# An attention and MLP kernel: other slots for the tile preparation, q turns ahead of their copies, and a last tile in three pieces

## The chip, the cores and the metric

The kernel runs on one core of a Trainium2 chip. The metric is the device time in microseconds (us), the median of several executions. All times below are in us unless marked ns.

## What is computed

Eight batches of attention without a softmax, each of 576 rows and 8 heads of 64, are normalised and go through a two-layer perceptron with a residual:

```python
kv = np.einsum('bhsd,bhse->bhde', k, v)
out = np.einsum('bhsd,bhde->bhse', q, kv)
rms = np.sqrt(np.mean(out * out, axis=-1, keepdims=True) + 1e-06)
x = (out / rms * g_norm)              # then heads side by side: (8, 576, 512)
xn = (x - mu) / np.sqrt(var + 1e-06) * g_ln
return x + np.maximum(xn @ w_ch1, 0.0) @ w_ch2     # 512 -> 2048 -> 512
```

The kernel computes in bf16 with f32 sums, and applies the 1/sqrt(var) of the second norm only at the end (`rstd`, in the output step), since it commutes with the relu.

## The kernel before, in words

**Work and tiles.** A batch has 576 rows: four row tiles of 128 (`main_tile`) and a remainder of 64. The remainders of two batches make one tile (`rem_tile`, made with the odd batch), and the four remainder tiles make a ninth block, "rem", computed last. A block of four tiles (512 rows) goes through the first product `mm1` (L391: 64 matmuls of 128x128 weights against 512 columns, with the relu on ScalarE, L404) and the second product `mm2` (L438, 16 matmuls for each of four row tiles, then `finish`, L420: the output step `o_sb` on VectorE, then two output DMAs on SP).

**Preparation of a tile** (class `Tile`, `plan_tile` L359). It comes in four parts, each put into a slot: first (`o`: four matmuls of q with kv, L259; `sq`: squares on ScalarE, L265; `red`: sum over the head on VectorE, L286), second two slots later (`root` on ScalarE L296, `inv`, `y`, `x`, `xc` on VectorE, L303, L291, L310, L320), third six slots after the first (`var`: the squares of the deviations on ScalarE, L328), and fourth the turn of xc into xT, the operand of `mm1` (L331): on TensorE with a copy on ScalarE for the early batches, by a transposing DMA on SP (L340) for batches 3 to 7.

**Slots and the order of work.** All engines run what they are given in the order of the program (`manual_schedule`, L62). `tick` (L460) counts slots: one slot is four matmuls of 512 columns, or as many of fewer columns as make the same work. Each `tick` first runs what `at` has put into its slot, in the order of the slot number and, where that is equal, in the order in which it was put there; then come the slot's own matmuls and their relu. Each block takes 16 slots of `mm1` and 16 of `mm2`, so batch b starts in slot s = 32 b. The preparation of batch b runs in the slots of batch b-1: `mm1` of b-1 is s-32 to s-17, `mm2` of b-1 is s-16 to s-1. The output step of the first of the four row tiles of `mm2` is emitted just ahead of slot s-12, the second ahead of s-8, the third ahead of s-4. The second product's sums `p2` have two PSUM buffers (`ps2`), the relu's inputs `p1` have three (`ps1`), the attention outputs two (`ps_out`, tag "ops").

For batches 3 to 7, `kv_of` of batch b is in slot s-39, and `turn_q_dma` in slot s-38: a copy of q on VectorE (L201) and one transposing DMA on SP (L203). Loads of later batches stand on GpSimd's queue.

**The start.** Batch 0 is special. Its kv comes from `kv_first`; its first two tiles are computed ahead of slot 0 in two halves of the heads (`half_o` L485, `half_sq`, `half_red`), with q turned on TensorE (`turn_groups`, L177) and copied out by ScalarE in the first half and by VectorE in the second; `fill` (L193) are matmuls on zeros. w1 and w2 arrive in four quarters each (`load_w1`, `load_w2`, GpSimd's queue). The first slots' products use the first two quarters of w1 (`mm1(0, ts, 1, 0, 8)` for tiles 0 and 1), slots 4 and 5 the third, 6 and 7 the fourth.

**The end.** The last row tile of the "rem" block is computed in two column halves (`split_last`), so that the output step and the output DMAs of the first half run beside the matmuls of the second; the two DMAs of each go out on SP and on ScalarE's queue.

Of the kernel before, what the change touches and what calls it, by code (L numbers as in the profile page):

```python
# [14 lines left out]
def kernel(  # L15
# [11 lines left out]
    nc = tc.nc  # L27
    f32 = mybir.dt.float32
    bf16 = mybir.dt.bfloat16
    AF = mybir.ActivationFunctionType  # L30
    ALU = mybir.AluOpType
    AX = mybir.AxisListType

    B, H, S, D = q.shape
    Dm = H * D
# [3 lines left out]
    nDe = Dh // 128  # L39
    HP = H // 2  # L40
# [11 lines left out]
    work = ctx.enter_context(tc.tile_pool(name="work", bufs=3))  # L52
# [4 lines left out]
    ps_out = ctx.enter_context(tc.psum_pool(name="ps_out", bufs=2))  # L57
    ps1 = ctx.enter_context(tc.psum_pool(name="ps1", bufs=3))
    ps2 = ctx.enter_context(tc.psum_pool(name="ps2", bufs=2))
# [7 lines left out]
    g_ln_sb = consts.tile([128, Dm], f32)  # L67
    gn_row = consts.tile([128, D], f32)
    identity = consts.tile([128, 128], bf16)
# [6 lines left out]
    kv_pack = [consts.tile([128, HP, 128], bf16, name=f"kv_pack{i}") for i in range(4)]  # L76
# [87 lines left out]
    qts, held, blks, rstds, m1s, q_ps = {}, {}, {}, {}, {}, {}  # L164
# [12 lines left out]
    def turn_groups(tp, i, h0, h1):  # L177
        groups = ((0, 2 * i), (0, 2 * i + 1)) if i < 2 else ((64, 2 * i - 4), (64, 2 * i - 3))
        if i == J:
            groups = ((0, J),)  # L180
        for h in range(h0, h1):
            for half, (p0, j) in enumerate(groups):
                nc.tensor.transpose(
                    tp[h % 2 * D:h % 2 * D + D, (h - h0) // 2, half * 64:half * 64 + 64],
                    q_in[0][p0:p0 + 64, h, j, :], identity[p0:p0 + 64, p0:p0 + 64])
        return 64 * len(groups)
# [162 lines left out]
    def rem_tile(b):  # L349
        mms = []  # L350
        for half, bb in enumerate((b - 1, b)):
            qt, kp = qts.pop(bb), held.pop(bb)
            mms.append((slice(half * 64, (half + 1) * 64),
                        lambda hp, qt=qt: qt[:, J, hp, :64], kp))
        if "rem" not in blks:
            blks["rem"] = new_block("rem", 1)
        return Tile(mms, blks["rem"], b // 2)

    def plan_tile(s, make, turn_at, on_pe):  # L359
        box = []  # L360

        def first():
            t = make()
            box.append(t)
            t.o()
            t.sq()
            t.red()

        def second():
            t = box[0]  # L370
            t.y()
            t.x()
            t.xc()

        def third():
            box[0].var()

        def fourth():
            box[0].turn(on_pe)

        at(s, first)
        at(s + 2, second)
        at(s + 6, third)
        at(turn_at, fourth)
# [28 lines left out]
    def mm2_part(b, ts, p2, de0, de1, c0=0, c1=Dm):  # L413
        for de in range(de0, de1):
            if de % 4 == 0:
                tick()
            nc.tensor.matmul(p2[:, c0:c1], lhsT=m1s[b][:, de, ts * 128:(ts + 1) * 128],  # L417
                             rhs=w2_sb[:, de, c0:c1], start=(de == 0), stop=(de == nDe - 1))

    def finish(b, ts, p2, c0=0, c1=Dm, both=False):  # L420
        o_sb = outp.tile([128, Dm], f32, tag="osb", name="o_sb")
        nc.vector.scalar_tensor_tensor(o_sb[:, c0:c1], in0=p2[:, c0:c1],  # L422
                                       scalar=rstds[b][:, ts:ts + 1],
                                       in1=blks[b][0][:, ts, c0:c1], op0=ALU.mult, op1=ALU.add)
        if b == "rem":
            dsts = [out[2 * ts + hf, :S_LO, :].rearrange("(p j) e -> j p e", j=JJ)[J]
                    for hf in range(2)]
        elif b == 0:
            dsts = [(out[b, :S_LO, :].rearrange("(p j) e -> j p e", j=JJ)[j] if ts < 2 else
                     out[b, S_LO:, :].rearrange("(p j) e -> j p e", j=J)[j - J])  # L430
                    for j in (2 * ts, 2 * ts + 1)]
        else:
            dsts = [out[b, :S_LO, :].rearrange("(p j) e -> j p e", j=JJ)[ts],
                    out[b, S_LO:, :].rearrange("(p j) e -> j p e", j=J)[ts]]
        nc.sync.dma_start(dsts[0][:, c0:c1], o_sb[:64, c0:c1])
        (nc.scalar if both else nc.sync).dma_start(dsts[1][:, c0:c1], o_sb[64:, c0:c1])

    def mm2(b, split_last=False):  # L438
        for ts in range(4):
            if split_last and ts == 3:  # L440
                for c0 in (0, Dm // 2):
                    p2 = ps2.tile([128, Dm], f32, tag="p2", name="p2")
                    mm2_part(b, ts, p2, 0, nDe, c0, c0 + Dm // 2)
                    finish(b, ts, p2, c0, c0 + Dm // 2, both=True)
                    del p2
            else:
                p2 = ps2.tile([128, Dm], f32, tag="p2", name="p2")
                mm2_part(b, ts, p2, 0, nDe)
                finish(b, ts, p2)
                del p2  # L450
        del blks[b], m1s[b]
# [5 lines left out]
    def at(slot, fn):  # L457
        agenda.setdefault(int(slot), []).append((slot, fn))
# [19 lines left out]
    t = [main_tile(0, i) for i in range(4)]  # L478
    for i in range(2):
        t[i].ss = work.tile([128, H, 1], f32, tag="ss", bufs=4, name="ss")  # L480
    sqs = [work.tile([128, H, D], f32, tag="sq", name="sq") for _ in range(2)]
    banks = (((ps_out, "ops"), (ps_m, "misc")), ((ps_out, "ops"), (ps1, "p1")))
    copies = ((nc.scalar.copy, nc.scalar.copy), (nc.vector.tensor_copy, nc.vector.tensor_copy))

    def half_o(half):  # L485
        hp0 = half * HP // 2
        tp = ps2.tile([128, 2, HP // 2, 128], bf16, tag="p2", name="tp")
        for i in range(2):
            turn_groups(tp[:, i], i, 2 * hp0, 2 * hp0 + H // 2)
            copies[half][i](qts[0][:, i, hp0:hp0 + HP // 2], tp[:, i])  # L490
        res = []
        for i in range(2):
            pool, tag = banks[half][i]
            o = pool.tile([128, H // 2, D], f32, tag=tag, name="o_half")
            flat = o.rearrange("p h e -> p (h e)")
            for k2 in range(HP // 2):
                nc.tensor.matmul(flat[:, k2 * 128:(k2 + 1) * 128], lhsT=qts[0][:, i, hp0 + k2, :],
                                 rhs=kv_pack[0][:, hp0 + k2, :], start=True, stop=True)
            res.append(o)
        return res  # L500

    def half_sq(i, half, o):
        nc.scalar.activation(sqs[i][:, half * H // 2:(half + 1) * H // 2], o, func=AF.Square)

    def half_red(i, half):
        hs = slice(half * H // 2, (half + 1) * H // 2)
        nc.vector.tensor_reduce(t[i].ss[:, hs], sqs[i][:, hs], axis=AX.X, op=ALU.add)

    oa = half_o(0)
    half_sq(0, 0, oa[0])  # L510
    half_sq(1, 0, oa[1])
    ob = half_o(1)
    half_sq(0, 1, ob[0])
    half_sq(1, 1, ob[1])
    for half in range(2):
        half_red(0, half)
    half_red(1, 0)
    half_red(1, 1)
    del oa, ob, sqs
    t[0].o_g(ps1, "p1")  # L520
    t[1].o_g(ps1, "p1")
    fill(5)
    t[0].x_g()
    t[1].root()
    x_blk, st, xT = t[0].blk
    for i in range(2):
        cs = slice(i * Dm // 2, (i + 1) * Dm // 2)
        xc = work.tile([128, Dm // 2], bf16, tag="xch", bufs=2, name="xc")
        nc.vector.scalar_tensor_tensor(xc, in0=x_blk[:, 0, cs], scalar=st[:, 1, 0:1],
                                       in1=g_ln_sb[:, cs], op0=ALU.add, op1=ALU.mult)  # L530
        tp = ps_out.tile([128, 2, 128], bf16, tag="ops", name="tp")
        for kk in range(2):
            nc.tensor.transpose(tp[:, kk, :], xc[:, kk * 128:(kk + 1) * 128], identity)
        nc.scalar.copy(xT[:, 2 * i:2 * i + 2, :128], tp)
        del xc, tp
    t[1].x_g()
    t[1].xc()


    def x2():  # L540
# [19 lines left out]
        load_batch(2)  # L560

    at(0, lambda: turn_first(2, ps_m, "misc"))
    at(2, lambda: t[1].turn(True))
    at(2.1, o2)
    at(2.2, x2)
    at(4, lambda: turn_first(3, ps_m, "misc"))
# [23 lines left out]

    at(21, lambda: kv_of(1))
    q_turns(23, 1)
    for j, s, tn in ((0, 24, 29), (1, 27, 34), (2, 31, 38), (3, 35, 42)):
        plan_tile(s, lambda j=j: main_tile(1, j), tn, True)
    at(46, lambda: rstd_of(1))

# [10 lines left out]
    for b in range(3, B):  # L607
        s = 32 * b
        if b > 3:
            at(s - 60, lambda b=b: load_batch(b, qts[b - 1][:1, J, HP - 1, 127:]))  # L610
            at(s - 39, lambda b=b: kv_of(b))
            at(s - 38, lambda b=b: turn_q_dma(b))
        for j in range(J):
            o = s - 28 + (0, 5, 10, 15)[j]
            plan_tile(o, lambda b=b, j=j: main_tile(b, j), o + 6, False)
        if b % 2:
            plan_tile(s - 11, lambda b=b: rem_tile(b), s - 5, False)
        at(s + 14, lambda b=b: rstd_of(b))
    at(32 * B + 14, lambda: rstd_of("rem"))

# [56 lines left out]
```

## Time and profile before

| what | value |
|---|---|
| median of 10 runs | 298.46 us (297.88 to 300.15) |
| the profiled execution's own time | 297.88 us |
| its span, first to last instruction | 296.10 us |
| mean granted TensorE clock | 0.998 |
| TensorE busy | 284.7 us |
| ScalarE, VectorE busy | 157.1, 149.6 us |
| DMA moved | 35.84 MB |

The time of one execution is its span and 1.78 us around it. In the lines of the profile, PE is TensorE's matmuls, PEld its weight loads, ACT is ScalarE, DVE VectorE, POOL GpSimd, SP SyncE; a "q" behind a name is the engine's queue issuing a DMA. L401 is line 401. A line of the timeline has the start and the length in us, engine, line, operation, what it writes and reads, shape, and how many alike are merged (x4); in brackets stands how long the engine sat idle before it and what ended that. The end of a matmul is modelled, so the distance of the starts is the better measure of TensorE's pace.

By that measure, before the first product starts (17.09) TensorE waits for the inputs, the q turns and the first tiles. The loop from batch 3 on takes about 30 us for each batch: batch 3's first product starts at 115.92, batch 4's at 145.74, batch 5's at 176.20, and the "rem" block's at 264.28. The last matmul ends at 292.11, the last output step at 292.63.

### The profile page before, as it was taken

What the parts mean: (1) busy time and instruction counts of PE and PEld (TensorE: products, weight loads), DVE (VectorE), ACT (ScalarE), POOL (GpSimd) and SP (SyncE); (2) the same over time, 40 slices, a digit from 0 to 9 for tenths busy, and PEclk for the clock granted to TensorE, in tenths of its full rate; (3) what the DMA queues carried; (4) which work ended last, traced back from release to release, by engine and by line L of the source; (5) the groups of instructions that cost most, each with busy time, mean ns of one, the idle gap of its engine ahead of it and who ended that gap; (6) DMA issues with size and microseconds to landing.
All of it is one profiled execution on the core that took longest, in us unless ns stands there. A gap on an engine that the chain in (4) does not pass through costs nothing.

```text
span 296.1 us, 5754 instructions
## 1 busy us (share of the span) xinstructions
PE 284.7 (96%) x2305; PEld 159.2 (54%) x2305; DVE 149.6 (51%) x332; ACT 157.1 (53%) x341; POOL 40.7 (14%) x68
## 2 busy tenths in 40 slices
PE   8879999999999999999999999999999899999994
PEld 3469854996569644445444544444444344444443
DVE  5657018936995794468246953692369500220022
ACT  3457754885559742784187417931793266016500
POOL 8523500032023000500050005000000000000000
PEclk9999999999999999999999999999999999999999
DMA  7999999459579926994799249966411330131033
GB/s 213 203 206 202 201 203 197 97 96 192 115 143 167 144 56 127 166 195 81 150 170 164 55 91 162 202 106 124 90 35 38 75 85 0 38 74 32 2 71 71
DMA packets 63130, 35.84 MB, mean 121 GB/s; under 512 B 30716, under 2 KB 58108, under 8 KB 63104
## 3 DMA queue, kind: packets, MB, share of 16 engines
q0 software_dynamic: 28016, 17.76, 42.2%
q1 hardware_dynamic: 34656, 16.99, 28.5%
q10 hardware_dynamic: 432, 0.72, 0.7%
q8 instruction: 18, 0.29, 0.4%
q14 instruction: 8, 0.07, 0.1%
HBM read 36.71 MB, written 9.44 MB: 156 GB/s over the span
## 4 chain that ended last, share of the span: by engine, by line
PE 72%; DVE 12%; DMA 7%; ACT 5%; issue 2%; SPq 1%; POOL 0%; DVEq 0%; POOLq 0%
PE p L401 38%; PE p L417 28%; DMA qt<-q_p 3%; DVE x_blk L310 2%; DVE y L291 2%; DMA v_in<-in_v_dram 2%; PE o_ps L259 2%; DVE o_sb L422 2%; ACT m L404 2%; DVE xc L320 1%; PE kv_ps L234 1%; DVE ss L286 1%; DMA xT_blk<-xc 1%; PE tp L336 1%; ACT dev L328 1%
## 5 line engine op out<-in xcount | busy, mean ns | idle before, releaser
L401 PE MATMUL p<-xT_blk,w_sb 128*128 128x128 bf16 (+2 forms) x1024 | 131.7, 286 | 1.0 <-ACT xT_blk L338 0.7
L417 PE MATMUL p<-w_sb,m 128*128 128x512 bf16 (+1 forms) x592 | 131.0, 374 | 1.4 <-DVE o_sb L422 1.4
L404 ACT ACTIVATE m<-p 128x512 bf16<-128x512 f32 x144 | 85.6, 597 | 66.0 <-PE p L401 64.7
L401 PEld LDWEIGHTS <-w_sb 128*128 128x128 bf16 x1024 | 78.5, 98 | 46.5 <-issue 1.9
L417 PEld LDWEIGHTS <-m 128*128 128x128 bf16 x592 | 56.2, 98 | 62.0 <-issue 2.3
L422 DVE SCALAR_TENSOR_TENSOR o_sb<-p,rstd,x_blk 128x512 f32<-128x512 f32 (+1 forms) x37 | 27.0, 732 | 43.1 <-PE p L417 40.4
L286 DVE TENSOR_REDUCE ss<-sq 128x8 f32<-128x512 f32 x34 | 23.2, 682 | 26.4 <-ACT sq L265 26.4
L328 ACT ACTIVATE dev<-x_blk,st_blk 128x512 f32<-128x512 f32 x36 | 25.8, 716 | 7.2 <-DVE st_blk L314 7.0
L265 ACT ACTIVATE sq<-o_ps 128x512 f32<-128x512 f32 x34 | 20.2, 595 | 15.5 <-PE o_ps L259 15.2
L320 DVE SCALAR_TENSOR_TENSOR xc<-x_blk,st_blk,g_ln_sb 128x512 bf16<-128x512 f32 x35 | 26.3, 752 | 1.2
L291 DVE TENSOR_TENSOR y<-o_ps,inv 128x512 f32<-128x512 f32 x34 | 23.5, 691 | 2.7
L310 DVE SCALAR_TENSOR_TENSOR x_blk<-y,g_norm_sb 128x512 f32<-128x512 f32 x34 | 23.5, 692 | 1.2
L410 DVE RECIPROCAL rstd<-rstd 128x4 f32<-128x4 f32 x9 | 1.6, 174 | 39.8 <-ACT rstd L409 39.8
L296 ACT ACTIVATE rms<-ss,eps_sb 128x8 f32<-128x8 f32 x36 | 10.8, 301 | 13.9 <-DVE ss L286 13.5
L303 DVE RECIPROCAL inv<-rms 128x8 f32<-128x8 f32 x36 | 7.2, 199 | 21.4 <-ACT rms L296 21.3
L98 POOL COPY gate<-qt 1x1 bf16<-1x1 bf16 x5 | 0.9, 177 | 123.2 <-DMA qt<-q_p 123.2
L259 PEld LDWEIGHTS <-qt 128*128 128x128 bf16 (+1 forms) x152 | 9.9, 100 | 8.3 <-issue 1.7
L259 PE MATMUL o_ps<-kv_pack,qt 128*128 128x128 bf16 (+1 forms) x152 | 13.3, 221 | 0.6 <-DMA qt<-q_p 0.6
L196 PE MATMUL p<-fill_sb 128*128 128x512 bf16 x29 | 8.3, 449 | 1.2 <-DVE eps_sb L137 1.2
L338 ACT COPY xT_blk<-tp 128x512 bf16<-128x512 bf16 x11 | 6.4, 582 | 3.5 <-PE tp L336 3.5
L328 ACT ACTIVATION_READ_ACCUMULATOR dev<-x_blk,st_blk 128x1 f32 x36 | 6.9, 192 | 0.0
L234 PEld LDWEIGHTS <-k_in 128*64 128x64 bf16 x280 | 5.4, 112 | 2.6 <-issue 2.5
(78 smaller groups left out, 115.9 us busy)
## 6 DMA issues: line engine op xcount, KB each, us to landing
out_dram<-o_sb SPq DMA_DIRECT2D x70, 128.0 KB, 2.4
w_sb<-in_moe_w_ch_dram POOLq DMA_DIRECT2D x8, 512.0 KB, 13.9
k_in<-in_k_dram POOLq DMA_DIRECT2D x7, 320.0 KB, 5.4
v_in<-in_v_dram POOLq DMA_DIRECT2D x7, 320.0 KB, 7.9
q_in<-in_q_dram POOLq DMA_DIRECT2D x7, 320.0 KB, 10.3
q_in<-in_q_dram POOLq DMA_DIRECT2D x8, 256.0 KB, 10.9
k_in<-in_k_dram POOLq DMA_DIRECT2D x7, 256.0 KB, 6.4
v_in<-in_v_dram POOLq DMA_DIRECT2D x7, 256.0 KB, 8.7
```

Source lines behind the costliest of these rows:

```text
L259: nc.tensor.matmul(flat[rows, hp * 128:(hp + 1) * 128], lhsT=lhsT_of(hp), rhs=kvp[:, hp, :], start=True, stop=True)
L265: nc.scalar.activation(self.sq_t, self.o_ps, func=AF.Square)
L286: nc.vector.tensor_reduce(self.ss, self.sq_t, axis=AX.X, op=ALU.add)
L291: nc.vector.tensor_mul(self.y_t, self.o_ps, self.inv().to_broadcast([128, H, D]))
L296: nc.scalar.activation(self.r, self.ss, func=AF.Sqrt, scale=1.0 / D, bias=eps_sb)
L310: nc.vector.scalar_tensor_tensor(x_blk[:, ts].rearrange("p (h d) -> p h d", h=H), in0=self.y_t, scalar=1.0, in1=g_norm_sb.to_broadcast([12 ...
L320: nc.vector.scalar_tensor_tensor(self.xc_t, in0=x_blk[:, self.ts], scalar=st[:, 1, self.ts:self.ts + 1], in1=g_ln_sb, op0=ALU.add, op1=ALU ...
L328: nc.scalar.activation(dev, x_blk[:, ts], func=AF.Square, bias=st[:, 1, ts:ts + 1], accum_out=st[:, 2, ts:ts + 1])
L401: nc.tensor.matmul(p1[:, i, :], lhsT=w1_sb[:, kk, de * 128:(de + 1) * 128], rhs=blk[2][:, kk, sl], start=(kk == 0), stop=(kk == nK - 1))
L404: nc.scalar.activation(m1[:, de0:de0 + per, sl], p1, func=AF.Relu)
L417: nc.tensor.matmul(p2[:, c0:c1], lhsT=m1s[b][:, de, ts * 128:(ts + 1) * 128], rhs=w2_sb[:, de, c0:c1], start=(de == 0), stop=(de == nDe - 1))
L422: nc.vector.scalar_tensor_tensor(o_sb[:, c0:c1], in0=p2[:, c0:c1], scalar=rstds[b][:, ts:ts + 1], in1=blks[b][0][:, ts, c0:c1], op0=ALU.mu ...
```

## The change

Four edits, all in the kernel's function:

1. The first two tiles. `half_turn` turns both tiles' q of one half into two PSUM tiles of their own, and the two copies follow; the products and squares are interleaved (`half_o(0, 0)`, second turns, `half_o(1, 0)` and so on), and the first root is taken ahead of the second tile's sums. x of the second tile is now also centred and turned in two column halves (`halves_xc`, `halves_turn`), in two buffers of the "ops" pool with two copies on ScalarE, where one "misc" buffer and one copy were.
2. The turn of batch 1's first tile is in slot 30, not 29.
3. For batches 3 to 7 the four tiles start in slots s-28, s-24, s-19, s-15 (were s-28, s-23, s-18, s-13), with the turn six slots later as before; the remainder tile starts in s-8 (was s-11), its turn in s-2 (was s-5).
4. The last row tile's columns come in 256, 128, 128 (were 256, 256).

```diff
     def mm2(b, split_last=False):
         for ts in range(4):
             if split_last and ts == 3:
-                for c0 in (0, Dm // 2):
+                for c0, c1 in ((0, 256), (256, 384), (384, Dm)):
                     p2 = ps2.tile([128, Dm], f32, tag="p2", name="p2")
-                    mm2_part(b, ts, p2, 0, nDe, c0, c0 + Dm // 2)
-                    finish(b, ts, p2, c0, c0 + Dm // 2, both=True)
+                    mm2_part(b, ts, p2, 0, nDe, c0, c1)
+                    finish(b, ts, p2, c0, c1, both=True)
...
-    def half_o(half):
+    def half_turn(half):
         hp0 = half * HP // 2
-        tp = ps2.tile([128, 2, HP // 2, 128], bf16, tag="p2", name="tp")
+        tps = [ps2.tile([128, HP // 2, 128], bf16, tag="p2", name="tp") for _ in range(2)]
         for i in range(2):
-            turn_groups(tp[:, i], i, 2 * hp0, 2 * hp0 + H // 2)
-            copies[half][i](qts[0][:, i, hp0:hp0 + HP // 2], tp[:, i])
-        res = []
+            turn_groups(tps[i], i, 2 * hp0, 2 * hp0 + H // 2)
         for i in range(2):
-            pool, tag = banks[half][i]
-            o = pool.tile([128, H // 2, D], f32, tag=tag, name="o_half")
-            flat = o.rearrange("p h e -> p (h e)")
-            for k2 in range(HP // 2):
-                nc.tensor.matmul(flat[:, k2 * 128:(k2 + 1) * 128], lhsT=qts[0][:, i, hp0 + k2, :],
-                                 rhs=kv_pack[0][:, hp0 + k2, :], start=True, stop=True)
-            res.append(o)
-        return res
-
-    def half_sq(i, half, o):
+            copies[half][i](qts[0][:, i, hp0:hp0 + HP // 2], tps[i])
+
+    def half_o(i, half):
+        hp0 = half * HP // 2
+        pool, tag = banks[half][i]
+        o = pool.tile([128, H // 2, D], f32, tag=tag, name="o_half")
+        flat = o.rearrange("p h e -> p (h e)")
+        for k2 in range(HP // 2):
+            nc.tensor.matmul(flat[:, k2 * 128:(k2 + 1) * 128], lhsT=qts[0][:, i, hp0 + k2, :],
+                             rhs=kv_pack[0][:, hp0 + k2, :], start=True, stop=True)
         nc.scalar.activation(sqs[i][:, half * H // 2:(half + 1) * H // 2], o, func=AF.Square)
...
-    oa = half_o(0)
-    half_sq(0, 0, oa[0])
-    half_sq(1, 0, oa[1])
-    ob = half_o(1)
-    half_sq(0, 1, ob[0])
-    half_sq(1, 1, ob[1])
-    for half in range(2):
-        half_red(0, half)
+    half_turn(0)
+    half_o(0, 0)
+    half_turn(1)
+    half_o(1, 0)
+    half_o(0, 1)
+    half_red(0, 0)
+    half_red(0, 1)
+    half_o(1, 1)
+    t[0].root()
     half_red(1, 0)
     half_red(1, 1)
-    del oa, ob, sqs
     t[0].o_g(ps1, "p1")
     t[1].o_g(ps1, "p1")
     fill(5)
     t[0].x_g()
     t[1].root()
-    x_blk, st, xT = t[0].blk
-    for i in range(2):
-        cs = slice(i * Dm // 2, (i + 1) * Dm // 2)
-        xc = work.tile([128, Dm // 2], bf16, tag="xch", bufs=2, name="xc")
-        nc.vector.scalar_tensor_tensor(xc, in0=x_blk[:, 0, cs], scalar=st[:, 1, 0:1],
-                                       in1=g_ln_sb[:, cs], op0=ALU.add, op1=ALU.mult)
-        tp = ps_out.tile([128, 2, 128], bf16, tag="ops", name="tp")
-        for kk in range(2):
-            nc.tensor.transpose(tp[:, kk, :], xc[:, kk * 128:(kk + 1) * 128], identity)
-        nc.scalar.copy(xT[:, 2 * i:2 * i + 2, :128], tp)
-        del xc, tp
+    def halves_xc(i):
+        x_blk, st, _ = t[i].blk
+        for c in range(2):
+            cs = slice(c * Dm // 2, (c + 1) * Dm // 2)
+            xc = work.tile([128, Dm // 2], bf16, tag="xch", bufs=4, name="xc")
+            nc.vector.scalar_tensor_tensor(xc, in0=x_blk[:, i, cs], scalar=st[:, 1, i:i + 1],
+                                           in1=g_ln_sb[:, cs], op0=ALU.add, op1=ALU.mult)
+            yield xc
+
+    def halves_turn(i, xcs, pool, tag):
+        xT = t[i].blk[2]
+        for c, xc in enumerate(xcs):
+            tp = pool.tile([128, 2, 128], bf16, tag=tag, name="tp")
+            for kk in range(2):
+                nc.tensor.transpose(tp[:, kk, :], xc[:, kk * 128:(kk + 1) * 128], identity)
+            nc.scalar.copy(xT[:, 2 * c:2 * c + 2, i * 128:(i + 1) * 128], tp)
+
+    halves_turn(0, halves_xc(0), ps_out, "ops")
     t[1].x_g()
-    t[1].xc()
+    xc1 = list(halves_xc(1))
...
-    at(2, lambda: t[1].turn(True))
+    at(2, lambda: halves_turn(1, xc1, ps_out, "ops"))
...
-    for j, s, tn in ((0, 24, 29), (1, 27, 34), (2, 31, 38), (3, 35, 42)):
+    for j, s, tn in ((0, 24, 30), (1, 27, 34), (2, 31, 38), (3, 35, 42)):
...
-            o = s - 28 + (0, 5, 10, 15)[j]
+            o = s - 28 + (0, 4, 9, 13)[j]
             plan_tile(o, lambda b=b, j=j: main_tile(b, j), o + 6, False)
         if b % 2:
-            plan_tile(s - 11, lambda b=b: rem_tile(b), s - 5, False)
+            plan_tile(s - 8, lambda b=b: rem_tile(b), s - 2, False)
```

## The prediction

> **What bounds the kernel now.** I read the page's busy table and clock row first, then TensorE's waits, then the timeline where those waits fall.
>
> ```profile
> span 296.1 us, 5754 instructions
> ...
> PE 284.7 (96%) x2305; PEld 159.2 (54%) x2305; DVE 149.6 (51%) x332; ACT 157.1 (53%) x341; POOL 40.7 (14%) x68
> ...
> PEclk9999999999999999999999999999999999999999
> ```
>
> TensorE sets the time, at full granted clock. Its work is the same before and after but for 16 more, smaller matmuls in the last tile, so what can move is its waits and the two ends. They are (engine, line, releaser: us in total, times, longest):
>
> ```profile
> PE p L417 <- DVE o_sb L422: 1.4, 3, 1.1
> PE tp L533 <- DVE xc L529: 1.2, 1, 1.2
> ...
> PE p L401 <- ACT xT_blk L338: 0.7, 1, 0.7
> PE o_ps L259 <- DMA qt<-q_p: 0.6, 2, 0.4
> ...
> PE tp L336 <- DVE xc L320: 0.2, 1, 0.2
> ```
>
> These understate: a 512-column matmul is recorded as 379 ns but starts every 216 ns (24 in 5.18 us in the chain), so a gap in the row starts is about 0.17 longer than the idle shown. In that measure batch 3's preparation costs 0.33 (row 112.18 below) + 0.29 (115.92, just after its rows end) + 0.39 (119.75); batch 5's 0.35 + 0.22 + 0.56 (172.53, 176.20, 180.21); batch 7's 1.26 + 0.22 (232.98, 236.65). Sum 3.62. Batches 4 and 6 cost nothing. Slot 29 (49.11) costs 0.25 + 0.17 = 0.42. TensorE around batch 3:
>
> ```profile
> 112.18 3.61 PE L417 MATMUL p<-w_sb,m 128*128 128x512 bf16 x16 [0.16 <-DVE o_sb L422]
> 115.92 3.61 PE L401 MATMUL p<-xT_blk,w_sb 128*128 128x512 bf16 x16
> 119.75 0.40 PE L259 MATMUL o_ps<-kv_pack,qt 128*128 128x128 bf16 x4 [0.22 <-DMA qt<-q_p]
> ```
>
> VectorE works strictly in order. Batch 4, third tile to the fourth (VectorE's timeline):
>
> ```profile
> 132.21 0.20 DVE L303 RECIPROCAL inv<-rms 128x8 f32<-128x8 f32 x1 [1.18 <-ACT rms L296]
> 132.51 0.69 DVE L291 TENSOR_TENSOR y<-o_ps,inv 128x512 f32<-128x512 f32 x1
> 133.24 0.69 DVE L310 SCALAR_TENSOR_TENSOR x_blk<-y,g_norm_sb 128x512 f32<-128x512 f32 x1
> ...
> 134.16 0.75 DVE L320 SCALAR_TENSOR_TENSOR xc<-x_blk,st_blk,g_ln_sb 128x512 bf16<-128x512 f32 x1
> 134.83 0.68 DVE L286 TENSOR_REDUCE ss<-sq 128x8 f32<-128x512 f32 x1
> 135.43 0.74 DVE L422 SCALAR_TENSOR_TENSOR o_sb<-p,rstd,x_blk 128x512 f32<-128x512 f32 x1
> 136.08 0.19 DVE L303 RECIPROCAL inv<-rms 128x8 f32<-128x8 f32 x1
> ```
>
> The row starts give the prices: inv to y 0.30, y to x 0.73, x to xc 0.92, xc to the next 0.67; ScalarE's root starts 0.72 after the reduction's start and 0.33-0.35 before inv. From a tile's root to VectorE free: 2.95. A tile with nothing between: 0.72 + 2.95 = 3.67. Four slots with one tile's o are 4 x 0.864 + 0.22 = 3.68. Spacing 4 just fits, with no room left over.
>
> **The change part by part.**
>
> *Tiles at s-28, s-24, s-19, s-15; remainder at s-8 and not s-11.* Nothing is added, all is order. The first output step (o_sb of the first row tile of the running second product) is emitted just before slot s-12; that product's third row tile, at slot s-8, needs its buffer back, since p2 has two. Before, the fourth tile's y, x, xc came at s-11, after that step: the row 135.43 stands ahead of the fourth tile's inv (136.08). Now they come at s-13, ahead of it. I replay batch 4 with 0 = start of its first o (119.75), s-28. ScalarE's relu of slot s-19 starts at 9.53 (one slot of matmuls and 0.20 after the third o at 8.24), then in order rstd 0.49 later, var 0.19 later, relu 0.71 later, root 0.48 later: 11.40 (before: 131.86 - 119.75 = 12.11). VectorE is then free of the second tile (its xc ends its turn at 10.01). So the third tile is done at 11.40 + 2.95 = 14.35; fourth: reduction there, root 15.07, done 18.02; o_sb 18.02 to 18.77. TensorE wants the buffer at four o (0.88) + 20 slots (17.28) = 18.16. It waits 0.65, and the rest of the product and the next batch stand behind it. Even batches (4, 6) pay that: 1.30. Odd ones (3, 5, 7) have the remainder's o at exactly that place (104.53 to 104.89 by starts, and 0.10 on the way in: 0.46), which covers all but 0.19: 0.57.
>
> What goes: the second output step is no longer behind the remainder's y, x, xc (111.39 stood behind those), so 0.33, 0.35, 1.26 go; the fourth tile's DMA transpose is issued before slot s-8, so 0.29, 0.22, 0.22 go.
>
> The q transpose (SP L203, which every tile turn and output DMA on SP passes or is passed by) stays near. From the start of the next batch's kv at slot s-7: casts end 1.66 later (108.45 to 110.11, two at 109.36 and 109.74); only then the remainder's root, 2.95 to the q_p copy at 4.61, which ends at 5.43; issue 5.48, SP's earlier output DMAs being out by then; transfer 5.00 (114.71 to 119.71 in the chain); usable 10.53. TensorE is there after 0.81 + 11 x 0.864 = 10.31: waits 0.22, twice (0.44), against 0.39 and 0.56. The remainder's own turn is now behind that 3.1 us issue; its xT is read a slot block later at the earliest (batch 7's: 34 slots), so nothing.
>
> Sum of the loop: 1.30 + 0.57 + 0.44 = 2.31 against 3.62: **-1.31**. Bounds: -3.2 if o_sb is never late, +1.2 if it is 0.5 later than I have it in all five batches.
>
> *Turn of batch 1's first tile at 30.* xc ends at 49.05; slot 30 starts 0.86 after the place that waited. ScalarE's copy (0.58, behind dev) ends about 51.4, and slot 32 needs it at 51.7. **-0.42**, bounds 0 and -0.42.
>
> *First two tiles.* The four waits on q copies (0.5, 0.4, 0.2, 0.2 in the waits view) mostly go. Replay: ScalarE copies at 10.22 and 10.48 (start distance 0.27, as 10.99 to 11.26), first o 10.64, second turns 10.80 to 11.25, VectorE copies to 11.69, last o 11.75, squares to 12.48, reductions 0.33 apart with the last at 12.91, first inv 13.24 against 14.33: the first xc is 1.09 earlier. But the second quarter of w1 stands in the way. Its DMA is issued at 6.04 and its landing is marked at 17.87; GpSimd's next issue, which waited for it, shows it:
>
> ```profile
> 18.15 0.68 POOL L94 DMA_DIRECT2D v_in<-in_v_dram  x1 [1.58 <-DMA w_sb<-in_moe_w_ch_dram]
> ```
>
> The second slot started at 18.02 before; it can start at 17.92. Of 1.09, 0.10 is left. Then tile 1 in halves adds one VectorE op (0.13 in all, hidden by that wait, which is its price if the wait were gone) and one ScalarE copy (two of 0.37 for one of 0.58), and takes both "ops" buffers: the third tile's o, which ran at 19.14, must now wait for the first copy (19.88), and slot 2's product behind it starts at 20.16 against 20.24. Its square starts 20.36 against 20.07, its xc ends 24.77 against 24.48, its turn waits 0.28, with slot 6 behind it. TensorE reaches the third tile's products at 26.84 against 26.74, where it waited before anyway: **+0.10**. Bounds: -0.7 if w1 lands earlier, +0.35.
>
> *Last tile in 256, 128, 128.* TensorE: 32 matmuls of 128 columns for 16 of 256. [...] I take 1.79: +0.04. VectorE's last step: 0.75 for 512 columns, 0.48 for 256, so an estimated 0.35 for 128: -0.13. The DMA: 128 KB lands in 2.4, 64 KB in 1.9 (SP) and 2.2 (ACT queue), so 32 KB maybe 0.2 sooner. [...] I take -0.11. **-0.20**, bounds +0.2 and -0.35.
>
> Sum: -1.31 - 0.42 + 0.10 - 0.20 = **-1.83**. The profiled execution took 297.88 with a span of 296.10; span 294.27, its time 296.05. The median of the ten runs is 0.58 above that execution: 298.46 - 1.83 = **296.6**.
>
> **The rivals.**
> - *o_sb is in time* (0.14): then 1.87 more goes: 294.8. For it: its lateness is a sum of eight row distances. Against it: each was taken from the same place one batch earlier.
> - *The head gives its second back* (0.10): w1 lands early enough, up to 0.7 more: 295.8. Against it: landing and use are 0.15 apart in this trace, and the DMA rows move about 200 GB/s without a break there.
> - *Slower: ScalarE falls behind at spacing 4* (0.16). Place: the relu chain of slots s-28 to s-17. By recorded durations four slots hold 4 x 0.60 + 0.60 + 0.30 + 0.91 = 4.21 of ScalarE against 3.68 of TensorE; by start distances (relu 0.49, dev 0.71) about 3.4. If the first is nearer, each tile adds 0.5, o_sb is some 0.9 later, five times 4.5: 301.1; half of it, 298.9. It decides from 1.83/5 = 0.37 later in each batch. Against it: spacing 5 has the same overload by durations (4.81 in 4.54) and shows no TensorE wait on ScalarE there.
> - *Hardly any change* (0.10): o_sb about 0.3 later than I have it, 298.1.
>
> **How the numbers follow.** My forecast has 0.50: 296.6, own range 296.0 to 297.5. 0.2% (0.60) is about what a measurement can tell here. Faster 0.74 (forecast, both gainers), same 0.14, slower 0.12 (most of the ScalarE case; its milder half counts as same). Range 294.7 to 298.6, from the first rival to the mild end of the slower one.
>
> **What would show it.** TensorE's wait on o_sb: five, about 0.5 idle in even batches at slot s-8, almost none in odd ones, none at s-4. In VectorE's rows o_sb of the first row tile stands after the fourth tile's xc. No wait on xT from a DMA; two short ones on qt. First xc near 14.5, but the second L401 slot no earlier than w1's landing; L336's wait at slot 29 gone. Wrong if even batches show no o_sb wait, if TensorE waits for ScalarE in L401, or if the first product ends over 0.5 earlier.

## The result, and the profile after

| | before | after |
|---|---|---|
| median | 298.41 us (51 runs) | 297.08 us (14 runs, 295.84 to 298.45) |
| ratio of the two, 95% interval | | 0.9948, 0.9936 to 0.996 |
| the profiled execution's own time | 297.88 | 295.75 |
| its span | 296.10 | 293.81 |

The change made the kernel faster: by 1.33 us in the median, by 2.29 in the span of the two profiled executions. The forecast was 296.6 for the median and 294.27 for the span. The difference between 1.33 and 2.29 is a finding of its own (experiments 4 and 5, and the table there).

The head of the page after, in the columns of the one shown of before:

```profile
span 293.8 us, 5804 instructions
...
PE 284.1 (97%) x2321; PEld 159.7 (54%) x2321; DVE 149.9 (51%) x334; ACT 157.9 (54%) x342; POOL 40.7 (14%) x68
...
PEclk9999999999999999999999999999999999999999
```

TensorE is busy nearly as long as before (284.1 for 284.7), with 16 more matmuls; what went is for the most part idle time. TensorE's waits after (engine, line, releaser: us in total, times, longest):

```profile
PE tp L539 <- DVE xc L530: 1.5, 1, 1.5
...
PE p L417 <- DVE o_sb L422: 0.9, 2, 0.5
PE p L401 <- DMA w_sb<-in_moe_w_ch_dram: 0.7, 1, 0.7
PE o_ps L259 <- ACT xT_blk L540: 0.7, 1, 0.7
PE o_half L499 <- ACT qt L491: 0.4, 1, 0.4
```

The waits on qt from a DMA and the one at slot 29 (L336) are no longer in the list. The wait on o_sb is now twice 0.46, at another slot than before, and a wait of 0.7 on w1 (`w_sb`) is new. TensorE's timeline shows the first at slot s-8 of batch 4, where the forecast put it, and the odd batch 3 without it:

```profile
106.70 0.42 PE L259 MATMUL o_ps<-kv_pack,qt 128*64 128x128 bf16 x8
107.22 1.02 PE L417 MATMUL p<-w_sb,m 128*128 128x512 bf16 x4
...
115.04 3.62 PE L401 MATMUL p<-xT_blk,w_sb 128*128 128x512 bf16 x16
118.60 0.40 PE L259 MATMUL o_ps<-kv_pack,qt 128*128 128x128 bf16 x4
...
137.40 1.02 PE L417 MATMUL p<-w_sb,m 128*128 128x512 bf16 x4 [0.46 <-DVE o_sb L422]
```

At 106.70 the remainder's o stands where batch 4 waits. VectorE's timeline tells why batch 4 waits at 137.40:

```profile
133.97 0.20 DVE L303 RECIPROCAL inv<-rms 128x8 f32<-128x8 f32 x1 [0.37 <-ACT rms L296]
134.28 0.69 DVE L291 TENSOR_TENSOR y<-o_ps,inv 128x512 f32<-128x512 f32 x1
135.01 0.69 DVE L310 SCALAR_TENSOR_TENSOR x_blk<-y,g_norm_sb 128x512 f32<-128x512 f32 x1
...
135.93 0.75 DVE L320 SCALAR_TENSOR_TENSOR xc<-x_blk,st_blk,g_ln_sb 128x512 bf16<-128x512 f32 x1
136.60 1.40 DVE L422 SCALAR_TENSOR_TENSOR o_sb<-p,rstd,x_blk 128x512 f32<-128x512 f32 x2
```

Before, the first o_sb (135.43) stood ahead of the fourth tile's inv (136.08); now it stands behind its xc, together with the second (x2). In the head, the chain of waits ("start, length, what", each step followed back to what released it) has a single piece from 6.04 to 17.79:

```profile
5.40 0.64 POOL q_in L132
6.04 11.75 DMA w_sb<-in_moe_w_ch_dram
17.79 0.05 issue
17.84 1.08 PE p L401 x16
```

In before the chain at this place ran through the q copies, the sums and xc of the first tile (ACT, PE and DVE pieces of 0.3 to 1.4 from 9.93 to 17.15), among them these:

```profile
13.01 1.40 DVE ss L507 x4
...
15.56 0.89 DVE xc L529 x2
...
17.15 1.94 PE p L401 x32
```

The last step on VectorE before, of 256 columns, and the last ones after, now of 128:

```profile
292.15 0.48 DVE L422 SCALAR_TENSOR_TENSOR o_sb<-p,rstd,x_blk 128x256 f32<-128x256 f32 x1 [1.26 <-PE p L417]
```

```profile
288.47 0.48 DVE L422 SCALAR_TENSOR_TENSOR o_sb<-p,rstd,x_blk 128x256 f32<-128x256 f32 x1 [1.00 <-PE p L417]
289.37 0.35 DVE L422 SCALAR_TENSOR_TENSOR o_sb<-p,rstd,x_blk 128x128 f32<-128x128 f32 x1 [0.41 <-PE p L417]
290.26 0.35 DVE L422 SCALAR_TENSOR_TENSOR o_sb<-p,rstd,x_blk 128x128 f32<-128x128 f32 x1 [0.54 <-PE p L417]
```

Where the 2.29 came from, read as the shift of each relu's start (ScalarE, L404) between the two traces, and of the ends:

| stage | forecast | measured |
|---|---|---|
| first two tiles: first slot 17.09 to 16.00, second 18.02 to 17.84, from slot 8 on | +0.10 | 0.00 |
| slot 30 (52.16 to 51.74) | -0.42 | -0.42 |
| loop, batches 3 to 7 | -1.31 | -1.51 |
| last tile, up to the end of the span | -0.20 | -0.36 |
| sum | -1.83 | -2.29 |

### The profile page after: what moved, and what is told of

It is laid out like the page before. It is cut to its first block, busy times and chain, and to the rows that moved or that the text cites. A ratio compares the mean times of both kernels' runs of the same rounds, so it can differ in the third digit from the quotient of the medians.

```text
span 293.8 us, 5804 instructions
## 1 busy us (share of the span) xinstructions
PE 284.1 (97%) x2321; PEld 159.7 (54%) x2321; DVE 149.9 (51%) x334; ACT 157.9 (54%) x342; POOL 40.7 (14%) x68
## 4 chain that ended last, share of the span: by engine, by line
PE 71%; DVE 11%; ACT 6%; DMA 6%; issue 4%; POOL 1%; DVEq 0%; SPq 0%; POOLq 0%
PE p L401 37%; PE p L417 29%; DMA w_sb<-in_moe_w_ch_dram 4%; DVE x_blk L310 3%; DVE y L291 3%; PE kv_ps L234 2%; PE o_ps L259 2%; DMA qt<-q_p 2%; ACT m L404 2%; DVE o_sb L422 1%; DVE xc L320 1%; ACT sq L265 1%; ACT dev L328 1%; DVE ss L286 1%; ACT rms L296 1%
## 5 line engine op out<-in xcount | busy, mean ns | idle before, releaser
L417 PE MATMUL p<-w_sb,m 128*128 128x512 bf16 (+2 forms) x608 | 130.8, 368 | 1.2 <-DVE o_sb L422 0.9
L404 ACT ACTIVATE m<-p 128x512 bf16<-128x512 f32 x144 | 84.8, 596 | 59.1 <-PE p L401 57.7
L422 DVE SCALAR_TENSOR_TENSOR o_sb<-p,rstd,x_blk 128x512 f32<-128x512 f32 (+2 forms) x38 | 26.9, 719 | 40.7 <-PE p L417 35.3
L320 DVE SCALAR_TENSOR_TENSOR xc<-x_blk,st_blk,g_ln_sb 128x512 bf16<-128x512 f32 x34 | 25.6, 752 | 1.2
L237 ACT CAST kv_pack<-kv_ps 64x256 bf16<-64x256 f32 x7 | 2.6, 365 | 8.9 <-PE kv_ps L234 8.8
```

The costliest lines, as they stand in the source:

```text
L320: nc.vector.scalar_tensor_tensor(self.xc_t, in0=x_blk[:, self.ts], scalar=st[:, 1, self.ts:self.ts + 1], in1=g_ln_sb, op0=ALU.add, op1=ALU ...
L404: nc.scalar.activation(m1[:, de0:de0 + per, sl], p1, func=AF.Relu)
```

## The experiments

Two theories of the loop stood against each other: the order on VectorE (a tile's y, x, xc ahead of an output step), and ScalarE too dense at a spacing of four slots. Of the head: w1's landing masks it, or the second tile's chain does.

**1. Each edit by itself.** Before with edit 3 only (`e1`), with edit 1 only (`e2`), with edit 4 only (`e3`).

```diff
# e1
-            o = s - 28 + (0, 5, 10, 15)[j]
+            o = s - 28 + (0, 4, 9, 13)[j]
-            plan_tile(s - 11, lambda b=b: rem_tile(b), s - 5, False)
+            plan_tile(s - 8, lambda b=b: rem_tile(b), s - 2, False)
```

> The kernel before with only the slots of batches 3 to 7 changed (s-28, s-24, s-19, s-15, remainder s-8). Theory (order on VectorE): the same waits as in the changed kernel from batch 3 on: o_sb in even batches 0.63 each at slot s-8 by matmul starts, in odd ones about 0.16, q transpose 0.1 to 0.3 twice, none on xT; the loop gives 1.5 us, span 294.6, time about 1.5 us under the kernel before. Rival (the edits work together, the loop gains only because the first tiles and slot 30 moved it): less than 1 us. Either way slot 29's wait (0.42) and the long last output stay.

> The kernel before with only the new first two tiles. Theory (w1's second quarter masks it): first xc about 14.48 in place of 15.56, the first product's second slot at 17.85 right after that landing, and from slot 8 on every matmul within 0.05 us of the kernel before; span 296.0 to 296.2, no change in time. Rival (the second won is lost elsewhere in the loop, not at the head): matmul starts at slots 4 to 12 about 1 us earlier than before.

> The kernel before with only the last tile in 256, 128, 128 columns. Theory: last output step 0.35 in place of 0.48, last output DMA 0.1 to 0.2 sooner; span 0.3 to 0.4 less, 295.75; last matmul within 0.05 of before. [...]

| edit alone | median (runs) | ratio to before, 95% | shift read in its trace |
|---|---|---|---|
| 3, loop | 297.34 (21) | 0.9969, 0.996 to 0.9978 | -1.11 |
| 1, first tiles | 298.56 (14) | 1.0013, 0.9998 to 1.0029 | 0.00 from slot 8 to the loop |
| 4, last tile | 298.1 (14) | 0.9994, 0.9981 to 1.0006 | -0.37 from the last relu to the end |

The last tile's gain is in the trace, but 0.3 to 0.4 is less than the medians can tell. The first tiles gain nothing by themselves: slot 1 starts at 17.83 in this trace too. Edit 3's -1.11 lies between what the expectation and its rival gave (1.5, and under 1), and is 0.40 short of what the edit shows in after: the o_sb waits are the same (0.63, 0.63, 0.16, 0.18, 0.18), but at the start of batch 3 the wait on qt is 0.51 and not 0.11. It comes from VectorE, in the remainder tile:

```profile
111.66 0.20 DVE L303 RECIPROCAL inv<-rms 128x8 f32<-128x8 f32 x1 [1.60 <-ACT rms L296]
112.34 0.69 DVE L291 TENSOR_TENSOR y<-o_ps,inv 128x512 f32<-128x512 f32 x1 [0.48 <-DVE inv L303]
```

y waits 0.48 behind its own inv, and the copy of q, which stands behind this tile's xc, with it. In after y starts 0.31 after inv at this place, 0.37 less than here. The same pause is in the trace of after too, 0.46 at 186.99 in a tile where nothing waits for it. In two traces (`e1`, `e4`) it fell on this remainder tile and in five on that later tile; why VectorE pauses, and what decides where, is open.

**2. The order on VectorE or ScalarE's load.** After with the fourth tile one slot later (`e4`: s-14, where before had s-13 and after has s-15), and after with only the fourth tile early, the second and third back at before's places (`e5`).

```diff
-            o = s - 28 + (0, 4, 9, 13)[j]
+            o = s - 28 + (0, 4, 9, 14)[j]      # e4
+            o = s - 28 + (0, 5, 10, 13)[j]     # e5
```

> The changed kernel with the fourth tile one slot later (s-14), so that its y, x, xc are emitted in slot s-12, just after the first output step and not just before it. Theory (order on VectorE): no wait on o_sb in any batch (0.63, 0.63, 0.16, 0.17, 0.17 gone), the fourth tile's xc only about 0.7 later, xT still in time; the q transpose's waits up to 0.2 longer each, since TensorE comes sooner; span about 1.4 less than the changed kernel, 292.4. Rival (ScalarE or VectorE as a whole is too slow at four-slot spacing): the waits remain, at most 0.2 smaller each, span over 293.3.

> The kernel after, with the tiles of batches 3 to 7 at s-28, s-23, s-18 and s-15: only the second and third are put back to where they were before, the fourth stays early. Theory (order on VectorE): the wait at slot s-8 is there because the fourth tile's y, x, xc stand ahead of the first output step on VectorE, and they are ready one third tile later; with the third tile one slot later the chain is up to 0.9 later, so the wait on o_sb grows from 0.63 to about 1.2 to 1.5 in even batches and from 0.17 to about 0.7 to 1.0 in odd ones, and the loop is 2 to 4 us longer than after's. Rival (ScalarE is too dense at spacing 4): more room between the tiles makes the wait shrink or vanish, and the loop is no longer than after's.

`e4`: 295.5 (5 runs), ratio 0.9905 (0.9892 to 0.9918), span 292.64. No wait on o_sb is left. VectorE's timeline of batch 4:

```profile
133.91 0.75 DVE L422 SCALAR_TENSOR_TENSOR o_sb<-p,rstd,x_blk 128x512 f32<-128x512 f32 x1
134.57 0.19 DVE L303 RECIPROCAL inv<-rms 128x8 f32<-128x8 f32 x1
...
137.36 0.75 DVE L422 SCALAR_TENSOR_TENSOR o_sb<-p,rstd,x_blk 128x512 f32<-128x512 f32 x1 [0.16 <-PE p L417]
```

One slot later in the program, and the output step is 2.7 earlier (133.91 for 136.60) because it is ahead of inv. `e5`: 300.17 (4 runs), ratio 1.0065 (1.0041 to 1.0088). Its TensorE timeline, batches 3 and 4:

```profile
108.99 1.02 PE L417 MATMUL p<-w_sb,m 128*128 128x512 bf16 x4 [0.84 <-DVE o_sb L422]
...
139.94 1.02 PE L417 MATMUL p<-w_sb,m 128*128 128x512 bf16 x4 [1.21 <-DVE o_sb L422]
```

More room between the tiles made the waits longer, each of the five batches by 0.68 to 0.70 against after, and the loop 3.8 longer (2 to 4 expected). ScalarE's density would have made them shorter. Taken with `e4` the order on VectorE is shown as the cause, and a spacing of four slots as harmless here.

**3. The remainder and the copy of q.** After with the remainder back at s-11 (`e6`), and `e4` with q's copy and transpose one slot earlier, ahead of the remainder's second part (`e9`).

```diff
-            plan_tile(s - 8, lambda b=b: rem_tile(b), s - 2, False)
+            plan_tile(s - 11, lambda b=b: rem_tile(b), s - 5, False)     # e6
-            at(s - 38, lambda b=b: turn_q_dma(b))
+            at(s - 39, lambda b=b: turn_q_dma(b))                        # e9
```

> The kernel after, with the remainder tile back at s-11 and its turn at s-5 (what the remainder's move is worth by itself). Theory: the remainder's o (0.46 of TensorE's time) goes away from the place just ahead of slot s-8, where it covered part of the wait in odd batches, so those wait at s-8 as the even ones do, about 0.6 against 0.17 (+0.4 in each of batches 3, 5, 7); its root, y, x and xc come back ahead of the second output step, so a wait of 0.1 to 0.35 at s-4 comes back in odd batches; the wait on qt at the next batch's start is about as long as in after (0.1 to 0.3). Together about 1 to 2 us longer than after. Rival (the remainder's move is worth nothing, the fourth tile's place does it all): within 0.3 of after.

> The kernel after with the fourth tile at s-14 (the run before this one with that edit had a span of 292.64 and waits on qt of 0.50 and 0.28, none on o_sb), and the copy of q and its transpose put one slot earlier, at s-39, ahead of the second part of the remainder tile on VectorE. Theory: q's copy stands behind the remainder's root, y, x and xc on VectorE (about 3), and that, not the transfer, makes qt late; ahead of them both waits go and the span is 291.8 to 292.1, the shortest runs about 293.7. Rival (the transposing DMA itself is the late one, or SP stands behind something): the waits stay within 0.2 of 0.50 and 0.28, span 292.4 to 292.7.

`e6`: 296.36 (8 runs), ratio 0.9949 (0.9932 to 0.9967). Within the loop its trace is 0.50 longer than after, less than expected and made otherwise. (The medians, 296.36 and 297.08, seem to say the opposite; among runs of full clock they are 296.35 and 295.86, see the table of experiment 5.) Odd batches did not get a longer wait at s-8: the remainder's o at s-11 also stands ahead of that slot, so its cover was never at stake, and that step of the expectation was wrong. Batches 3 and 5 lost their qt waits (0.11 and 0.25 gained), and batch 7 alone pays, 0.87 at s-4:

```profile
232.90 3.61 PE L417 MATMUL p<-w_sb,m 128*128 128x512 bf16 x16 [0.72 <-DVE o_sb L422]
```

So of edit 3, the remainder's move is worth 0.50, taken with the new places of the tiles. `e9`: 294.88 (4 runs), ratio 0.9886 (0.9871 to 0.9901). No wait on qt or o_sb is left in its list; from the first relu of batch 2 to the last one its loop is 2.09 shorter than after's, 3.60 shorter than before's, which is the 3.62 of stalls that the prediction had counted. The expected span and shortest run were missed all the same (294.30 for at most 292.1, 294.68 for 293.7): the mean clock of all four runs was 0.994 or less, which is the subject of experiment 5. q's copy was late because of the order on VectorE, not because of its transfer.

**4. What masks the head.** After without the load of 160 KB that stands ahead of w1's second quarter (`e7`), and after with the two loads exchanged (`e12`).

```diff
-    nc.gpsimd.dma_start(q_in[0][64:, :, :J], up(q, 0))        # e7: left out, zeros in its place
     load_w1(1)
+    nc.gpsimd.dma_start(q_in[0][64:, :, :J], up(q, 0))        # e12: here
...
-    at(0, lambda: turn_first(2, ps_m, "misc"))
+    at(2, lambda: turn_first(2, ps_m, "misc"))                # e12
```

> The kernel after, without the load of the upper half of batch 0's q (160 KB; zeros stand in its place, so the rows of batch 0 that come from it are not computed), which stands on GpSimd's queue ahead of the second quarter of w1. Theory: the head's gain of 1.08 at the first product is masked by the landing of that quarter (17.79, slot 1 at 17.84). With 160 KB less ahead of it the quarter lands about 1 to 1.5 sooner, slot 1 starts right behind slot 0 at about 16.9 to 17.0, and slot 8 and all after it come 0.5 to 0.9 sooner than in after. Rival (it is the second tile's chain that decides, not w1): slot 1 is earlier but from slot 2 or 8 on there is no gain.

> The kernel after with two loads on GpSimd's queue exchanged: the second quarter of w1 ahead of the upper half of batch 0's q, and the turn of that half (third tile) in slot 2 in place of slot 0. Theory: w1's quarter, which lands at 17.8 in after, is what masks the head's gain; now it lands near 16.5, slot 1 starts behind slot 0 at about 16.9 (17.84), and slot 8 and all behind it come 0.3 to 0.9 sooner: less than without the load, since the turn of the third tile now stands in front of its o in slot 2. Shortest runs 295.0 to 295.5 (after 295.84). Rival (the third tile decides): slot 1 sooner but slot 8 where it was or later, shortest runs 295.8 to 296.3.

`e7`: 294.82 (6 runs), ratio 0.9896 (0.9871 to 0.9922). TensorE's timeline has the 32 matmuls of slots 0 and 1 without a break, and from the second slot's on every relu is 0.96 to 0.98 earlier than in after (0.5 to 0.9 expected), to the end (its line numbers are one lower):

```profile
15.93 1.99 PE L400 MATMUL p<-xT_blk,w_sb 128*128 128x128 bf16 x32
17.76 0.39 PE L538 MATMUL tp<-identity,xc 128*128 128x128 bf16 x4
```

The second that the first tiles gain is real, and the landing of w1 hid it. `e12`, which computes everything, has the 32 matmuls without a break too, though in its trace at half clock:

```profile
16.26 3.75 PE L401 MATMUL p<-xT_blk,w_sb 128*128 128x128 bf16 x32
```

Its shortest runs are 295.54 to 295.62, 0.26 less than after's and short of the expected 295.0 to 295.5. What takes the rest of the second there was not separated; the turn of the third tile, now ahead of its o in slot 2, is a candidate. Its median is 297.45 (9 runs; ratio to before 0.9955, 0.9935 to 0.9975). Six of its nine runs are 1.9 above the other three, which leads to the next question.

**5. Why the runs come in groups.** Each execution's mean granted clock is listed. Grouped by it, with the medians in us and the number of runs, the profiled ones among them; before's are the runs that were taken beside the experiments:

| kernel | clock 0.997 or more | 0.992 to 0.994 | 0.985 to 0.989 |
|---|---|---|---|
| before (93 runs) | 297.91 (36) | 298.49 (52) | 299.21 (5) |
| after | 295.86 (5) | 297.10 (8) | 298.37 (2) |
| `e1`, loop alone | 296.70 (3) | 297.33 (14) | 298.00 (4) |
| `e2`, first tiles alone | 297.96 (7) | 299.00 (6) | 300.36 (1) |
| `e3`, last tile alone | 297.48 (4) | 298.25 (8) | 298.93 (2) |
| `e4`, fourth tile at s-14 | 294.41 (1) | 295.51 (4) | |
| `e5`, wider spacing | 299.69 (2) | 300.74 (2) | |
| `e6`, remainder at s-11 | 296.35 (5) | 297.57 (3) | |
| `e7`, without a load | 294.82 (5) | 297.05 (1) | |
| `e9`, q's copy earlier | | 294.77 (3) | 296.11 (1) |
| `e12`, loads exchanged | 295.60 (3) | 297.52 (6) | |
| `e10`, after with more fill | 295.79 (6) | | |
| `e13`, before with more fill | 297.86 (5) | 299.35 (12) | |
| `e11`, all together | 293.50 (5) | | |

The trace of `e6` is one of a middle run (stretch: length, TensorE busy with count, granted clock, DMA share, GB/s):

```profile
9.62:13.03 3.41, 2.82 (x92) 1.00 1.28 203
13.03:16.44 3.41, 1.81 (x25) 1.00 1.31 205
16.44:19.86 3.42, 3.42 (x39) 0.50 1.25 207
19.86:23.27 3.41, 2.69 (x54) 1.00 1.24 207
```

For one stretch of 3.41 us, a half window in what follows, TensorE ran at half clock; 1.71 lost of 295.4 is a mean of 0.994, and two such stretches 0.988. (For runs without a trace the stretches are inferred from these means.) The clock rose at 6.20 in this trace and fell at 16.44, three times 3.413 later; in the trace of `e5` it rose at 4.10 and fell at 17.75, four times. In the fourteen traces the first rise lies anywhere from 3.89 to 6.89. Counted from it in windows of 3.413, the first six windows of each trace have a granted clock of 1.00 or of 0.50, so each change in them lies whole multiples of 3.413 behind the rise. In the seven traces that have a half window, the one ahead of the first holds 1.74 (`e12`) to 2.47 us (`e1`) of TensorE's recorded work. So little work alone was not enough, since three windows with 1.81 or 1.82 (after, `e2`, `e4`) were followed by full clock. What decides between these is open.

With the old head the half window came at 11.47, 12.56 and 13.72 (`e1`, `e13`, `e3`), over q turns and waits; with the new head at 16.44 to 17.75 (`e5`, `e6`, `e9`, `e12`), over the first products. By the table it costs 0.58 in before, 1.04 with edit 1 alone, 1.24 in after; that its place is the reason fits, but was not tested by itself. To test that the idle stretches are the cause, `e10` fills those of after, and `e13` those behind the q turns of before:

```diff
-    fill(5)
+    fill(10)
...
+    at(1, lambda: fill(3))       # e10 only
     at(2, ...)                   # the second tile's turn
+    at(2.05, lambda: fill(3))
```

> The kernel after, with 10 fill matmuls in place of 5 ahead of the first xc, and 3 more ahead of slot 1 and 3 behind the second tile's turn at slot 2, all in places where TensorE idles (1.65, 0.73 and 0.72 us). Theory: the runs of after at 297.1 rather than 295.8 are those in which the idle stretches of the new head take TensorE's granted clock to one half for one window of 3.4 us; with TensorE busy there, no such window comes, and all runs lie at about 295.8 to 296.1, median 296.0 (1.1 below after's median, ratio to before about 0.992). Rival (the clock drops come from elsewhere, or from windows further ahead): the same clusters as after, median 297.1, or more if the fills run at half clock and stand in the way (up to +2).

> The kernel before with 10 fill matmuls in place of 5 ahead of the first xc and 3 more behind the second tile's turn in slot 2, so that TensorE does not idle there. Theory (idle in the head costs some runs a window of 3.4 us at half clock): all runs at about 297.8 to 298.0, median 297.9 against 298.4 without, ratio about 0.998; then the change is worth 2.0 to 2.1 between kernels that both keep the clock, and 0.6 to 0.7 of that is lost in the medians. Rival (before's scatter from 297.8 to 299.2 comes from elsewhere): the same scatter, median 298.4.

`e10`: 295.79, all six runs between 295.69 and 295.84; ratio 0.9917 (0.99 to 0.9933). None of the six lost the clock, against 10 of 15 in after. Its windows hold more work:

```profile
11.15:14.56 3.41, 3.36 (x36) 1.00 1.33 203
14.56:17.97 3.41, 2.89 (x44) 1.00 1.24 206
17.97:21.39 3.42, 3.34 (x52) 1.00 1.25 207
```

`e13` missed: 299.12 (17 runs), ratio 1.0019 (1.0005 to 1.0034), slower. 12 of 17 runs lost the clock, 57 of 93 without the fill. In its trace the window ahead of the halving lies ahead of the added fill, among the waits for the q copies, and the fill runs at half clock and delays what follows:

```profile
9.15:12.56 3.41, 2.11 (x87) 1.00 1.28 204
12.56:15.98 3.42, 3.36 (x24) 0.50 1.33 204
```

**6. Together.** `e11` is after with the edits of `e4`, `e9` and `e12`, `fill(10)`, and three fills behind the second tile's turn.

> The kernel after with the edits that the runs before this one support, together: fourth tile at s-14, q's copy and transpose at s-39, the second quarter of w1 ahead of the upper half of q with that half's turn in slot 2, 10 fill matmuls in place of 5, and 3 more behind the second tile's turn. Theory (each stands for itself: loop -2.1 against after, exchanged loads -0.3, no half-clock window): span 291.4 to 291.7, all runs at about 293.2 to 293.6, median 293.4, ratio to before about 0.983. Rival (the fills don't hold the clock at this head's own timing, or the gains overlap): runs spread from 293.3 to 295.5, median above 294.2.

293.5 us (5 runs, 293.42 to 294.18), ratio 0.9847 (0.9833 to 0.9861): faster than both kernels, with no half window in any run. The profiled run is the longest, 294.18; in it all is 0.69 later than in after already at slot 2, where TensorE had waited 0.7 for the first v.

## Why the prediction was right, point by point

**The wait on o_sb** (the first output step behind the fourth tile's y, x, xc). Replayed at 0.65 in even and 0.19 in odd batches; measured by starts 0.63, 0.63 and 0.16, 0.17, 0.17. Counted from the first o of batch 4's preparation in after (118.60), the replay puts o_sb at 136.62 and TensorE's next matmuls at 137.41; the rows have 136.60 and 137.40. The mechanism is shown by `e4` and `e5`, and the remainder's o covers it in odd batches as said (106.70 above).

**What goes.** None of the waits at s-4 nor of those on xT from a DMA is left, as counted. The two on qt are 0.11 and 0.25 for 2 x 0.22. What is left of the loop's stalls is 2.12 for 2.31; the loop's -1.51 for -1.31 is these small terms added up.

**Slot 30.** -0.42, exact.

**First two tiles.** The replay gave the first inv at 13.24 (13.25 measured) and slot 1 held by w1 at 17.92 (17.84). `e7` shows that mask. The third tile's wait for its buffer is there as well (its o at 19.85, 19.88 in the replay), but it does not cost the 0.10: slot 2 began 0.17 earlier (20.07 for 20.24), the third tile's turn came 0.18 later (24.72 for 24.54) and not 0.28, and from 27.73 on TensorE's rows are the same in both. Here the sum of the steps was off by 0.10.

**Last tile.** The sum's DMA term is the one that was mis-sized. The output step took 0.35 as estimated (-0.13), and TensorE lost 0.04 as taken. The 1.79 behind that is what 32 matmuls of 128 columns took in the chain of before:

```profile
24.94 1.79 PE p L401 x32
```

From the output step of the 256 columns to the last one it is 1.75 in before, for 16 matmuls (290.40 to 292.15), and 1.79 in after, for 32 (288.47 to 290.26). The 0.11 taken for the DMA is shown by no run and was the author's estimate; in its place the DMA view of after shows 0.1 from issue to landing, 32 KB in 1.8 (SP) and 2.1 (ScalarE's queue) where 64 KB take 1.9 and 2.2. The rest behind the last output step became 0.27 shorter, not 0.11: from the last issue to SP's sight of the landing 2.25 became 2.08, and what comes behind it, the end of the program, 1.19 became 1.09. Sum -0.36 for -0.20.

**From the span to the median.** This step failed in its size. The prediction carried before's distance from profiled execution to median, 0.58, over to after; it was 1.33 (297.08 - 295.75). The profiled executions of both kernels are ones without a half-clock window, and the change raised the price of such a window from 0.58 to 1.24 while leaving it about as common (57 of 93 runs, 10 of 15). Compared at equal clock the change is worth 2.05 without a window, 1.39 with one. The forecast of 296.6 was 0.5 too low. That it was no further off is in part luck: the profiled execution's time was forecast 0.30 too high (296.05 for 295.75) and the distance from it to the median 0.75 too small, and these errors have opposite signs.

**The rivals.** "o_sb in time" fell: the waits are there. "The head gives its second back" fell for the stated reason, w1's landing, and `e7` shows what it would have been, 0.97 (the prediction had up to 0.7). "ScalarE falls behind" fell with `e5`, and no product of the loop waits for ScalarE. "Hardly any change" fell with the ratio's interval.

## What to carry to other kernels

A step that is moved ahead in an engine's order delays what it overtakes (here o_sb on VectorE by 2.7, 133.91 in `e4` and 136.60 in after): replay that engine's queue by the distances of its row starts, which gave the waits on o_sb to within 0.03 here, and ask of each overtaken step who waits for it. Where a gain ends at a transfer's landing, it isn't gone: look which load stands ahead of that transfer (here 160 KB, worth 0.96 to 0.98 in `e7`). And compare executions of equal granted clock before a median is explained: a half window at the start had a price, which here was 0.58 with one order of the start and 1.24 with another, and with fills in the idle time of after's start (`e10`) none of six runs paid it.

## What the runs showed of the hardware

- The granted clock went to one half for one or two stretches of 3.41 us in 10 of 15 executions of after (by their mean clocks, 0.988 to 0.994; `e6` and `e9` show one and two such stretches in their traces), whose longest idle stretch at that place was 1.5 us (the first row of after's waits). With matmuls on zeros in these stretches, the mean clock was 0.997 or more in all 11 runs of `e10` and `e11`.
- Fills in before's head did not keep the clock (12 of 17 runs of `e13` lost it) and cost time: with 10 of them in place of 5, a half window there costs 1.49 (299.35 to 297.86) for 0.58.
- Halving an output DMA from 64 to 32 KB shortened its way by about 0.1 in after (2.2 to 2.1 on ScalarE's queue, 1.9 to 1.8 on SP's: the DMA view's medians from issue to landing).
- A pause of VectorE between inv and y, with inv named as what y waited for: 0.48 in `e1` and `e4`, in the remainder tile of batch 3, and 0.46 in after, `e6`, `e7`, `e10` and `e12`, in a later tile (186.99 in after); none in the seven other traces. Its cause is open.
